# Fourteen value products for twenty, a turn moved from VectorE to TensorE in one batch, and splits on VectorE alone in another

## Chip, core and metric

The kernel runs on one core of a Trainium2 chip. The metric is the device time of one execution in microseconds (us); lower is better. TensorE is called PE, VectorE DVE, ScalarE ACT, GpSimd POOL, SyncE SP (its queue issues the DMAs).

## The reference

Three layers in a row, on 4 batches of 448 tokens. A causal attention with 12 heads of 64 columns; a mixing layer; and a second causal attention by 4 experts of which each token takes two.

```python
attn = softmax(causal(scale * q @ k.T)); x = attn @ v          # 12 heads, joined to 768 columns
theta = x @ w_theta
zr, zi = x * cos(theta), x * sin(theta)
u = x + w_tok_r @ zr + w_tok_i @ zi                            # over the 448 tokens
x = u + relu(u @ w_ch)
logits = x @ w_gate                                            # 4 experts, the best two are kept
for e in range(4):
    a = softmax(causal(scale * (x @ wq[e]) @ (x @ wk[e]).T))
    out += gate[e] * (a @ (x @ wv[e])) @ wo[e]
```

## The kernel before

Activations stand as features by tokens: six tiles `xt` of 128 x 448 per batch. Products that need accuracy are made of three: an operand is split into a rounded part and a rest, and hi x hi, hi x lo and lo x hi are added up in PSUM. So each of the big products of a batch (theta, channel, queries and keys) is 18 matrix instructions on 448 columns (`big`, line 877).

A batch runs through four stages: `attn1` (line 852, six pairs of heads), `mixing` (884), `project` (957: channel product, queries and keys, values with the gate's logits) and `attn2` (1052, two pairs of experts). `ORDER` (565) names the stages of all batches in the order in which they are recorded.

In `attn1` and `attn2` a pair of heads is a `Pair` (704). `scores` and `last` make the scores with queries on the partitions; DVE subtracts the mask and finds the row maximum, ACT takes the exponential, and ACT or POOL multiplies by the reciprocal sum. The result P lies in `pa` (2,048 columns: 16 blocks of 128 x 128, the causal part only). The values need P with keys on the partitions, so `turn` (772) turns it into `ph`: either PE transposes the 16 blocks into PSUM in four quarters of 512 columns and DVE or ACT copies each quarter out, or DVE transposes 32 x 32 blocks in place (two instructions of 1,024 columns) and 16 DMAs move the blocks. `BYDVE` (563) says for which pairs DVE does it. Then `two` (798, the loop at 828) multiplies by the values, query block by query block: 20 products a pair, 12 of 128 columns and 8 of 64. Each is two PE instructions, since these are plain 32-bit products.

Weights come as pairs of 32-bit halves of 64-bit numbers. In the first batch `widen` (641) makes them into a rounded part and a rest, by integer operations on DVE, a rounding copy on ACT, POOL or DVE, and a subtraction on POOL or DVE; the result is kept in DRAM (`scr`) and loaded as `unit` tiles by the later batches. There are six `unit` buffers and three `vt` buffers (values of the first attention). The seven tiles of token weights `wt` are widened in the first batch and stay. `split` (698) makes the two parts of an activation.

No engine's order is written by hand. Every operation is recorded with its due time, and `issue` (373) takes on each engine the recorded step that is due first and whose buffers are free. PE's own order comes from the table `RUNS` (568): so many steps of such a place of the program, then so many of another. `K` (566) holds the weights with which due times are worked out. A step recorded with a choice of engines (`copy`, `scale`, `combine`: letters s, v, g for ACT, DVE, POOL) goes to the one that would end it first. All are written out in `_emit` (537), so line 552 stands in nearly every row of the profile, and groups are told apart by tile names.

Of the kernel before, what the change touches and what calls it, by code (L numbers as in the profile page):

```python
# [17 lines left out]
OP = mybir.AluOpType  # L18
AX = mybir.AxisListType

B, H, S, D = 4, 12, 448, 64
DM = H * D
E = 4
P = 128
NK = DM // P
CW = [128, 128, 128, 64]
# [528 lines left out]
class Engine:  # L555
# [4 lines left out]
        return lambda *a, **kw: self._plan.add(self._name, method, *a, **kw)  # L560


BYDVE = {"a0": (), "a1": (3, 5, ), "a2": (0, 1, 2, 4, ), "a3": (0, 1, 2, 4, ), "c0": (0, 1, ), "c1": (0, ), "c2": (0, 1, ), "c3": ()}
ZBYDVE = [(), (), (), ()]
ORDER = ["a0", "m0", "a1", "p0", "c0", "m1", "a2", "p1", "c1", "m2", "a3", "p2", "c2", "m3", "p3", "c3"]
K = {"path": 1.7343403, "hop": 432.5379, "slack": -45.1941614, "war": 150.0, "ahold": 57315.6931, "free": -2869.0478,
    "warm": 16}
RUNS = [(1,2), (0,2), (2,1), (8,2), (3,4), (4,16), (14,1), (3,12), (5,1), (7,2), (9,1), (6,1), (14,1), (21,1),
# [23 lines left out]

# [3 lines left out]
def dense_sparse_attention_kernel(ctx: ExitStack, tc: tile.TileContext, qk, v, w64, w32, wo, wvg, wtok, out):  # L596
# [6 lines left out]
    plan = Plan(nc, tc)  # L603
    pe, act, dve, pool, sp = (Engine(plan, n) for n in ("tensor", "scalar", "vector", "gpsimd", "sync"))
# [14 lines left out]
    ident = const([P], F32, "ident")  # L619
# [21 lines left out]
    def widen(raw, n, hi, lo, by=1.0):  # L641


        e_, r_ = raw[:, :n, 1], raw[:, :n, 0].bitcast(U32)
        act.activation(e_.f32(), e_.f32(), AF.Copy, scale=REBIAS)
        e_ = e_.bitcast(U32)
        p_ = sbt([S], F32, "cmb")[:, :n]
        u_ = p_.bitcast(U32)
        dve.tensor_scalar(u_, e_, 3, 0x7FFFFFFF, op0=OP.logical_shift_left, op1=OP.bitwise_and)
        plan.claim(hi)  # L650
        dve.scalar_tensor_tensor(u_, r_, 29, u_, op0=OP.logical_shift_right, op1=OP.bitwise_or)
        dve.scalar_tensor_tensor(u_, e_, 0x80000000, u_, op0=OP.bitwise_and, op1=OP.bitwise_or)
        if by == 1.0:
            plan.copy(hi, p_, "sgv")
            plan.combine(lo, p_, hi.f32(), OP.subtract, "gv")
        else:
            plan.scale(hi, p_, by, "sgv")
            dve.scalar_tensor_tensor(lo, p_, by, hi.f32(), op0=OP.mult, op1=OP.subtract)
# [36 lines left out]
        parts = [t.rearrange("p h (k j) -> p h k j", j=width) for t in unit(u, DM // 2 if per == 2 else NVG, per, "unit")]  # L695
        return lambda a, k: parts[k // (NK // per)][:, a, k % (NK // per)]

    def split(dst_h, dst_l, src):
        plan.copy(dst_h, src, "svg")
        plan.combine(dst_l, src, dst_h.f32(), OP.subtract, "gv")  # L700

    UNIT = [14, 10, 0, 6]

    class Pair:

# [4 lines left out]
        def part(self, j, c):  # L710
            at = UNIT[c] + (c + 1) * j if c < 3 else UNIT[c]
            if self.by_dve:
                return self.by_key[:, at:at + c + 1]
            return self.p_[:, at * P:at * P + (128 * (c + 1) if c < 3 else S)]

        def softmax(self, sc_, p, n, m, col):
# [55 lines left out]
        def turn(self):  # L772
            plan.next()
            p_ = self.p_
            self.pt = pt = sbt([2048], F32, "ph")
            if self.by_dve:
                for at in (0, 1024):
                    dve.transpose(p_[:, at:at + 1024], p_[:, at:at + 1024])
                for a in range(4):
                    plan.group()  # L780
                    for b_ in range(4):
                        sp.dma_start(pt[32 * b_:32 * b_ + 32, 512 * a:512 * a + 512], p_[32 * a:32 * a + 32, 512 * b_:512 * b_ + 512])
                    plan.end_group()
            else:
                for i in range(4):
                    tp = pst("tp")
                    for n in range(4 * i, 4 * i + 4):
                        pe.transpose(tp[:, P * (n - 4 * i):P * (n - 4 * i + 1)], p_[:, P * n:P * n + P], ident)
                        if n == 4 * i:
                            plan.claim(pt)  # L790
                    plan.copy(pt[:, 512 * i:512 * i + 512], tp)

        def moving(self, at, q, n):
            if self.by_dve:
                return self.pt.rearrange("p (a u q) -> p a u q", a=4, u=16)[:, q // 32:(q + n) // 32, at]
            return self.pt[:, at * P + q:at * P + q + n]

    def two(pairs):

# [23 lines left out]
        for i, x in enumerate(pairs):  # L823
            plan.next()
            o_ = pst("tp")
            hl = [sbt([S], F32R, "hc") for _ in range(2)] if x.dest is None else []
            plan.group()
            for c in (2, 3, 1, 0):
                n = CW[c]
                for kc in range(c + 1):  # L830
                    for j in range(2):
                        if c == 3:
                            m = pairs[j].moving(UNIT[3] + kc, 64 * i, 64)
                        else:
                            m = x.moving(UNIT[c] + (c + 1) * j + kc, 0, P)
                        pe.matmul(o_[64 * j:64 * j + 64, c * P:c * P + n], x.vts[j][:, kc], m, start=(kc == 0), stop=(kc == c))
            plan.end_group()
            plan.completes(o_[:, :S])
            for tile_ in hl if x.dest is None else (x.dest,):
# [4 lines left out]
            h_, l_ = hl  # L844
# [39 lines left out]
    def mixing(b):  # L884
        hs = []
        xt = [x0[b, m] for m in range(NK)]
        for m in range(NK):
            t = sbt([2, S], F32R, "zt")
            h_, l_ = t[:, 0], t[:, 1]
            split(h_, l_, xt[m])  # L890
            hs.append((h_, l_))
        if b == 0:
            for k in range(7):
# [63 lines left out]
    def project(b):  # L957
        xt = [x0[b, m] for m in range(NK)]
        us = []
        for m in range(NK):  # L960
            t = sbt([2, S], F32R, "zt")
            split(t[:, 0], t[:, 1], xt[m])
            us.append((t[:, 0], t[:, 1]))
        for m in range(NK):
            o = big(6 + m, us)
# [3 lines left out]
        for m in range(NK):  # L969
            t = sbt([960], F32R, "zt")  # L970
            hi, lo = t[:, 0:S], t[:, 512:]
            split(hi, lo, xt[m])
            plan.combine(t[:, S:512], xt[m][:, 384:S], t[:, 384:S].f32(), OP.subtract, "gv")
            hs.append((hi, lo))
            both.append(t[:, 384:512])
        v2, qps = [], []
# [147 lines left out]
```

## Time and profile before

| | |
|---|---|
| three timed runs | 611.20, 611.82 (median), 612.81 us |
| the profiled execution's own time | 612.39 us |
| its span, first to last instruction | 610.6 us |
| busy: PE, DVE, ACT, POOL | 594.3, 419.9, 320.9, 126.8 us |
| mean granted clock of PE | 0.989 |
| instructions: PE, DVE, ACT, POOL | 4318, 1264, 862, 217 |

The time outside the span is 612.39 - 610.6 = 1.79 us. A granted clock of 1.00 is full speed. PE's instructions are pipelined, so the busy time of a stretch is the time in which any of them is under way.

### The profile page before, as it was taken

What the parts mean: (1) busy time and instruction counts of PE and PEld (TensorE: products, weight loads), DVE (VectorE), ACT (ScalarE), POOL (GpSimd) and SP (SyncE); (2) the same over time, 40 slices, a digit from 0 to 9 for tenths busy, and PEclk for the clock granted to TensorE, in tenths of its full rate; (3) what the DMA queues carried; (4) which work ended last, traced back from release to release, by engine and by line L of the source; (5) the groups of instructions that cost most, each with busy time, mean ns of one, the idle gap of its engine ahead of it and who ended that gap; (6) DMA issues with size and microseconds to landing.
All of it is one profiled execution on the core that took longest, in us unless ns stands there. A gap on an engine that the chain in (4) does not pass through costs nothing.

```text
span 610.6 us, 12498 instructions
## 1 busy us (share of the span) xinstructions
PE 594.3 (97%) x4318; PEld 515.8 (84%) x4318; DVE 419.9 (69%) x1264; ACT 320.9 (53%) x862; POOL 126.8 (21%) x217
## 2 busy tenths in 40 slices
PE   8999978999998999999999999999999999999987
PEld 6787866898897988988888887988898899999876
DVE  6999999999856876657454878648623976335360
ACT  6999887546554555145664676314634542200363
POOL 3554122521210324022020212302400201100020
PEclk9999996999998999999999999999999999999999
DMA  8457882379758756486586874456656756147442
GB/s 331 153 155 261 291 309 72 100 247 318 235 138 306 209 138 208 113 261 193 155 247 186 295 226 136 123 168 203 204 159 212 241 156 203 50 158 211 130 148 91
DMA packets 58622, 118.18 MB, mean 194 GB/s; under 512 B 8640, under 2 KB 22080, under 8 KB 58560
## 3 DMA queue, kind: packets, MB, share of 16 engines
q1 hardware_dynamic: 58560, 117.39, 61.0%
q8 instruction: 34, 0.56, 0.4%
q14 instruction: 28, 0.23, 0.1%
HBM read 80.37 MB, written 21.26 MB: 166 GB/s over the span
## 4 chain that ended last, share of the span: by engine, by line
PE 87%; ACT 6%; DVE 4%; issue 1%; DMA 1%; SPq 0%; POOL 0%; POOLq 0%; DVEq 0%; ACTq 0%
PE mm L552 61%; PE tp L552 27%; ACT pa L552 5%; DVE pa L552 2%; DVE cmb L552 1%; DMA unit<-scr 1%; DVE st L552 1%; ACT ph L552 0%; SPq L552 0%; DVE xt L552 0%; DVE zt L552 0%; ACT c L552 0%; DVE ph L552 0%; DVE tp L552 0%; ACT zt L552 0%
## 5 line engine op out<-in xcount | busy, mean ns | idle before, releaser
L552 PE MATMUL mm<-zt,unit 128*128 128x448 f32 x1152 | 244.2, 369 | 0.5 <-DVE zt L552 0.5
L552 PEld LDWEIGHTS mm<-zt,unit 128*128 128x128 f32 x1152 | 214.1, 188 | 25.4 <-issue 4.2
L552 ACT ACTIVATE pa<-pa,st 128x128 f32<-128x128 f32 (+4 forms) x229 | 110.1, 517 | 46.9 <-DVE st L552 45.5
L552 POOL TENSOR_SCALAR pa<-pa,st 128x128 f32<-128x128 f32 (+4 forms) x114 | 59.7, 540 | 220.1 <-DVE st L552 160.6
L552 PE MATMUL mm<-wt,zh 128*128 128x448 f32 x336 | 99.7, 376 | 4.9 <-DVE zt L552 3.5
L552 ACT ACTIVATE pa<-tp,st 128x128 f32<-128x128 f32 (+3 forms) x105 | 51.9, 505 | 42.5 <-DMA unit<-scr 17.9
L552 PEld LDWEIGHTS mm<-wt,zh 128*128 128x128 f32 x336 | 63.2, 192 | 11.6 <-issue 4.6
L552 PE MATMUL tp<-raw 64*128 64x256 f32 (+3 forms) x512 | 68.3, 438 | 0.2 <-DVE st L552 0.2
L552 PE MATMUL tp<-ph,vt 128*64 128x128 f32 (+1 forms) x1280 | 64.7, 258 | 2.1 <-DMA unit<-scr 2.1
L552 PEld LDWEIGHTS tp<-ph,vt 128*64 128x64 f32 x1280 | 57.7, 140 | 10.5 <-issue 3.7
L552 PE MATMUL mm<-wt,zl 128*128 128x448 f32 x168 | 62.4, 371 | 0.0
L552 PEld LDWEIGHTS tp<-raw 64*128 64x128 f32 (+1 forms) x512 | 38.3, 173 | 22.7 <-issue 8.7
L552 DVE CUSTOM_DVE_ANT_0 tp<-tp,mask 128x128 f32<-128x128 f32 (+3 forms) x105 | 45.6, 472 | 11.5 <-PE tp L552 10.4
L552 DVE CUSTOM_DVE_ANT_0 pa<-tp,mask 128x256 f32<-128x256 f32 (+3 forms) x119 | 47.2, 446 | 7.3 <-PE tp L552 6.9
L552 PE MATMUL tp<-ident,pa 128*128 128x128 f32 x272 | 36.2, 282 | 4.0 <-ACT pa L552 3.2
L552 DVE STREAM_TRANSPOSE pa<-pa 128x1024 f32<-128x1024 f32 x30 | 36.0, 1225 | 5.9 <-ACT pa L552 3.3
L552 PEld LDWEIGHTS tp<-ident,pa 128*128 128x128 f32 x272 | 31.1, 144 | 9.3 <-ACT pa L552 4.6
L552 POOL TENSOR_TENSOR zt<-xt,zt 128x448 fp32r<-128x448 f32 (+1 forms) x28 | 27.6, 999 | 53.5 <-DVE zt L552 48.4
L552 DVE SCALAR_TENSOR_TENSOR xt<-mm,xt 128x448 f32<-128x448 f32 x24 | 14.9, 623 | 34.3 <-PE mm L552 34.3
L552 DVE TENSOR_TENSOR zt<-xt,zt 128x448 fp32r<-128x448 f32 (+1 forms) x68 | 35.0, 553 | 0.5
L552 ACT ACTIVATE zh<-tp 128x512 fp32r<-128x512 f32 (+1 forms) x37 | 18.6, 545 | 30.4 <-PE tp L552 30.4
L552 PEld LDWEIGHTS mm<-wt,zl 128*128 128x128 f32 x168 | 32.0, 191 | 2.9 <-DVE zl L552 0.3
(104 smaller groups left out, 714.6 us busy)
## 6 DMA issues: line engine op xcount, KB each, us to landing
unit<-scr SPq DMA_DIRECT2D x96, 384.0 KB, 4.0
ph<-pa SPq DMA_DIRECT2D x240, 64.0 KB, 2.0
scr<-unit SPq DMA_DIRECT2D x32, 384.0 KB, 3.3
raw<-qk SPq DMA_DIRECT2D x24, 448.0 KB, 5.6
c<-w SPq DMA_DIRECT2D x24, 384.0 KB, 4.1
vt<-v SPq DMA_DIRECT2D x24, 256.0 KB, 4.2
unit<-scr SPq DMA_DIRECT2D x18, 260.0 KB, 3.5
out<-cmb SPq DMA_DIRECT2D x18, 224.0 KB, 2.6
```

Of the source, the lines that this page charges most:

```text
L552: getattr(getattr(self.nc, engine), name)(*args, **kw)
```

## The change

- `BYDVE`: pairs 3 and 5 of the second batch's first attention are turned by PE (before: DVE); of its second attention both pairs are turned by DVE (before: the first alone).
- The values: a pair's three full query blocks are taken together. For key block 0 one product covers 384 columns, for block 1 256, for block 2 128, and the last query block keeps its four of 64: 7 products for each of the two heads, 14 in all. For that the 16 blocks lie in another order in `pa` and `ph` (`LAND`, `TURNS`, `KEYED`).
- In the first batch the subtractions of `split` and of `widen` are DVE's alone.
- `RUNS` and `K` are new, so all engines' orders change.

```diff
-BYDVE = {"a0": (), "a1": (3, 5, ), "a2": (0, 1, 2, 4, ), "a3": (0, 1, 2, 4, ), "c0": (0, 1, ), "c1": (0, ), "c2": (0, 1, ), "c3": ()}
+BYDVE = {"a0": (), "a1": (), "a2": (0, 1, 2, 4, ), "a3": (0, 1, 2, 4, ), "c0": (0, 1, ), "c1": (0, 1), "c2": (0, 1, ), "c3": ()}
-K = {"path": 1.7343403, "hop": 432.5379, "slack": -45.1941614, "war": 150.0, "ahold": 57315.6931, "free": -2869.0478,
+K = {"path": 1.6514121, "hop": 476.4898, "slack": -38.9360047, "war": 176.7037, "ahold": 44547.6112,
...
-RUNS = [(1,2), (0,2), (2,1), (8,2), (3,4), (4,16), (14,1), (3,12), (5,1), (7,2), (9,1), (6,1), (14,1), (21,1),
+RUNS = [(0,2), (1,2), (2,1), (8,2), (3,16), (7,2), (4,16), (9,1), (6,1), (5,1), (11,16), (14,2), (10,1), (22,1),
...
-            plan.combine(lo, p_, hi.f32(), OP.subtract, "gv")
+            plan.combine(lo, p_, hi.f32(), OP.subtract, "v")
...
-    def split(dst_h, dst_l, src):
+    def split(dst_h, dst_l, src, by="gv"):
         plan.copy(dst_h, src, "svg")
-        plan.combine(dst_l, src, dst_h.f32(), OP.subtract, "gv")
+        plan.combine(dst_l, src, dst_h.f32(), OP.subtract, by)
...
+    TURNS = [((1, 4, 6, 9), (1, 11), 5, slice(0, 4, 3)), ((10, 11, 14, 15), (0, 16), 4, slice(2, 4)),
+             ((0, 2, 3, 5), (0, 6), 3, slice(0, 3, 2)), ((7, 8, 12, 13), (4, 14), 5, slice(3, 5))]
...
-                for i in range(4):
+                for ats, (lo, hi), width, pick in TURNS:
                     tp = pst("tp")
-                    for n in range(4 * i, 4 * i + 4):
+                    for n, at in enumerate(ats):
...
-                    plan.copy(pt[:, 512 * i:512 * i + 512], tp)
+                    plan.copy(to, tp.rearrange("p (x y q) -> p x y q", x=2, y=2))
...
-            for c in (2, 3, 1, 0):
-                n = CW[c]
-                for kc in range(c + 1):
-                    for j in range(2):
...
+            for kc in range(3):
+                for j in range(2):
+                    pe.matmul(o_[64 * j:64 * j + 64, kc * P:384], x.vts[j][:, kc], x.moving(kc, j, kc, 384 - kc * P), start=(kc == 0), stop=(kc == 2))
+            for kc in range(4):
+                for j in range(2):
+                    pe.matmul(o_[64 * j:64 * j + 64, 384:S], x.vts[j][:, kc], pairs[j].moving(3, j, kc, 64, 64 * i), start=(kc == 0), stop=(kc == 3))
...
-            split(h_, l_, xt[m])
+            split(h_, l_, xt[m], "gv" if b else "v")
```

What the order of instructions shows of it at three places (tile numbers are those of the program; a row with x2 is two products). First PE, the values of the first pair of heads; before:

```order
L552 MATMUL tp_304<-ph_212,vt_102 64x128 x6
L552 MATMUL tp_304<-ph_212,vt_102 64x64
L552 MATMUL tp_304<-ph_226,vt_102 64x64
...
L552 MATMUL tp_304<-ph_212,vt_102 64x64
L552 MATMUL tp_304<-ph_226,vt_102 64x64
L552 MATMUL tp_304<-ph_212,vt_102 64x128 x6
```

and now:

```order
L552 MATMUL tp_320<-ph_279,vt_102 64x384 x2
L552 MATMUL tp_320<-ph_279,vt_102 64x256 x2
L552 MATMUL tp_320<-ph_279,vt_102 64x128 x2
L552 MATMUL tp_320<-ph_211,vt_102 64x64
L552 MATMUL tp_320<-ph_279,vt_102 64x64
...
L552 MATMUL tp_320<-ph_211,vt_102 64x64
L552 MATMUL tp_320<-ph_279,vt_102 64x64
```

The first two products now read columns of all three full query blocks. Second PE, the first two products of the first batch's mixing (`mm` from `wt` and the turned `zh`, `zl`; three instructions for each of the seven token weights); before:

```order
L552 MATMUL mm_1376<-wt_1266,zh_1160 128x448 x2
L552 MATMUL mm_1376<-wt_1266,zl_1161 128x448
...
L552 MATMUL tp_1355<-ident_67,pa_1248 128x128 x3
L552 MATMUL tp_1426<-ident_67,pa_1248 128x128 x4
L552 MATMUL tp_1435<-ident_67,pa_1248 128x128 x4
L552 MATMUL mm_1445<-wt_1266,zh_1229 128x448 x2
L552 MATMUL mm_1376<-wt_1266,zh_1160 128x448 x2
L552 MATMUL mm_1376<-wt_1266,zl_1161 128x448
```

and now:

```order
L552 MATMUL mm_1367<-wt_1294,zh_1174 128x448 x2
L552 MATMUL mm_1367<-wt_1294,zl_1175 128x448
L552 MATMUL tp_1376<-ph_1311,vt_796 64x384 x2
...
L552 MATMUL tp_1404<-raw_725 128x256
...
L552 MATMUL tp_1412<-raw_969 128x384
...
L552 MATMUL mm_1367<-wt_1294,zh_1174 128x448
L552 MATMUL mm_1436<-wt_1294,zh_1189 128x448 x2
...
L552 MATMUL tp_1469<-ph_1275,vt_1134 64x384 x2
```

Scores (from `raw`) and values (from `ph`) of the second batch's first attention now stand after the first token weight's products, ahead of those of the seventh. Third SP's queue, at the end of the first batch's projection (`scr` from `unit` stores a widened tile, `unit` from `scr` loads one for the second batch); before:

```order
L552 DMA scr_5_463_2407<-unit_2323 256x1x260
L552 DMA c_464_2417<-wo 128x256
L552 DMA vt_2456<-v 128x512
L552 DMA unit_2462<-scr_0_185_919 128x768
L552 DMA unit_2469<-scr_1_189_944 128x768
```

and now:

```order
L552 DMA scr_5_474_2361<-unit_2352 256x1x260
L552 DMA unit_2423<-scr_0_104_494 128x768
L552 DMA unit_2434<-scr_1_172_807 128x768
L552 DMA unit_2455<-scr_0_210_998 128x768
```

The values `vt` of the last pairs are loaded earlier, and the second batch's first units follow the last store directly.

## Rows read from the trace of the kernel before

**Rows 1.** The page's head: span, busy share of each engine, DVE in 40 slices

```profile
span 610.6 us, 12498 instructions
...
PE 594.3 (97%) x4318; PEld 515.8 (84%) x4318; DVE 419.9 (69%) x1264; ACT 320.9 (53%) x862; POOL 126.8 (21%) x217
...
DVE  6999999999856876657454878648623976335360
```

**Rows 2.** Stretches: length, busy time (instructions) by engine, granted clock, DMA share, GB/s

```profile
0.00:40.00 40.00, 37.08 (x364) 27.64 (x365) 34.52 (x155) 34.51 (x112) 19.94 (x48) 1.00 0.67 231
...
87.30:100.00 12.70, 6.79 (x29) 4.51 (x26) 12.46 (x31) 9.43 (x24) 4.74 (x8) 0.73 0.45 159
...
187.10:195.48 8.38, 6.29 (x62) 4.45 (x61) 5.58 (x30) 3.73 (x13) 0.73 (x1) 0.80 0.97 326
195.48:586.75 391.27, 391.27 (x2734) 346.61 (x2738) 239.21 (x692) 170.76 (x458) 63.55 (x106) 1.00 0.60 182
586.75:591.87 5.12, 3.54 (x20) 2.29 (x20) 4.63 (x31) 3.02 (x9) 0.59 (x2) 1.00 0.81 265
```

**Rows 3.** Timeline of DVE, two stretches: start, us, instruction

```profile
58.60 0.55 DVE L552 SCALAR_TENSOR_TENSOR unit<-cmb,unit 128x384 fp32r<-128x384 f32 x1
59.07 0.55 DVE L552 SCALAR_TENSOR_TENSOR cmb<-c,cmb 128x384 uint32<-128x384 uint32 x1
...
104.59 0.62 DVE L552 TENSOR_TENSOR wt<-cmb,wt 128x448 fp32r<-128x448 f32 x1
105.13 0.55 DVE L552 SCALAR_TENSOR_TENSOR cmb<-c,cmb 128x384 uint32<-128x384 uint32 x1
```

**Rows 4.** Timeline of SP's queue and PE, 187.2 to 192.0 us

```profile
187.34 0.40 SPq L552 DMA_DIRECT2D vt<-v  x1
...
187.83 3.14 SPq L552 DMA_DIRECT2D unit<-scr  x6
...
191.90 0.38 PE L552 MATMUL tp<-ph,vt 128*64 128x128 f32 x2 [2.09 <-DMA unit<-scr]
```

**Rows 5.** The chain that ended last, in order of time: start, us, what

```profile
191.90 3.58 PE tp L552 x40
...
264.22 3.85 PE mm L552 x18
268.06 1.50 PE tp L552 x12
...
505.65 0.77 PE tp L552 x7
...
510.67 1.93 PE tp L552 x40
...
541.61 32.93 PE mm L552 x162
```

**Rows 6.** Groups of instructions by shape: count, busy us, mean ns of one, idle before

```profile
L552 PE MATMUL tp<-ident,pa 128*128 128x128 f32 x272 | 36.2, 282 | 4.0 <-ACT pa L552 3.2 <-POOL pa L552 0.8
...
L552 DVE STREAM_TRANSPOSE pa<-pa 128x1024 f32<-128x1024 f32 x30 | 36.0, 1225 | 5.9 <-ACT pa L552 3.3 <-DMA unit<-scr 2.2 <-POOL pa L552 0.4
...
L552 POOL TENSOR_TENSOR zt<-xt,zt 128x448 fp32r<-128x448 f32 x20 | 23.6, 1189 | 38.8 <-DVE zt L552 33.7 <-ACT zt L552 4.9
...
L552 DVE COPY ph<-tp 128x512 f32<-128x512 f32 x21 | 13.5, 679 | 0.5 <-PE tp L552 0.5
```

**Rows 7.** Timeline of POOL and DVE side by side, 109.0 to 114.3 us

```profile
109.14 1.17 POOL L552 TENSOR_TENSOR zt<-xt,zt 128x448 fp32r<-128x448 f32 x1
...
109.85 4.59 DVE L552 TENSOR_TENSOR zt<-zt,xt 128x448 f32<-128x448 f32 x6
...
110.62 1.19 POOL L552 TENSOR_TENSOR zt<-xt,zt 128x448 fp32r<-128x448 f32 x1 [0.32 <-ACT zt L552]
```

**Rows 8.** DMA issues: count, KB each, median us from issue to landing

```profile
unit<-scr SPq DMA_DIRECT2D x96, 384.0 KB, 4.0
...
vt<-v SPq DMA_DIRECT2D x24, 256.0 KB, 4.2
```

More of the change, by code (lines that the diff above doesn't have):

```diff
@@ L560, in __getattr__ @@
         return lambda *a, **kw: self._plan.add(self._name, method, *a, **kw)
-BYDVE = {"a0": (), "a1": (3, 5, ), "a2": (0, 1, 2, 4, ), "a3": (0, 1, 2, 4, ), "c0": (0, 1, ), "c1": (0, ), "c2": (0, 1, ), "c3": ()}
+BYDVE = {"a0": (), "a1": (), "a2": (0, 1, 2, 4, ), "a3": (0, 1, 2, 4, ), "c0": (0, 1, ), "c1": (0, 1), "c2": (0, 1, ), "c3": ()}
 ZBYDVE = [(), (), (), ()]
 ORDER = ["a0", "m0", "a1", "p0", "c0", "m1", "a2", "p1", "c1", "m2", "a3", "p2", "c2", "m3", "p3", "c3"]
-K = {"path": 1.7343403, "hop": 432.5379, "slack": -45.1941614, "war": 150.0, "ahold": 57315.6931, "free": -2869.0478,
-    "warm": 16}
-RUNS = [(1,2), (0,2), (2,1), (8,2), (3,4), (4,16), (14,1), (3,12), (5,1), (7,2), (9,1), (6,1), (14,1), (21,1),
[23 rows of a table removed]
+K = {"path": 1.6514121, "hop": 476.4898, "slack": -38.9360047, "war": 176.7037, "ahold": 44547.6112,
+    "free": -864.6802, "warm": 16}
+RUNS = [(0,2), (1,2), (2,1), (8,2), (3,16), (7,2), (4,16), (9,1), (6,1), (5,1), (11,16), (14,2), (10,1), (22,1),
[23 rows of a table added]
 @with_exitstack
@@ L696, in load_unit @@
         return lambda a, k: parts[k // (NK // per)][:, a, k % (NK // per)]
-    def split(dst_h, dst_l, src):
+    def split(dst_h, dst_l, src, by="gv"):
         plan.copy(dst_h, src, "svg")
-        plan.combine(dst_l, src, dst_h.f32(), OP.subtract, "gv")
+        plan.combine(dst_l, src, dst_h.f32(), OP.subtract, by)
     UNIT = [14, 10, 0, 6]
+    LAND = {(2, 0, 2): 1, (2, 0, 1): 4, (2, 1, 1): 6, (2, 0, 0): 9, (2, 1, 2): 10, (3, 0, 0): 11, (2, 1, 0): 14, (3, 0, 1): 15,
+            (3, 0, 2): 0, (3, 0, 3): 2, (1, 0, 1): 3, (1, 1, 1): 5, (0, 0, 0): 7, (1, 0, 0): 8, (0, 1, 0): 12, (1, 1, 0): 13}
+    TURNS = [((1, 4, 6, 9), (1, 11), 5, slice(0, 4, 3)), ((10, 11, 14, 15), (0, 16), 4, slice(2, 4)),
+             ((0, 2, 3, 5), (0, 6), 3, slice(0, 3, 2)), ((7, 8, 12, 13), (4, 14), 5, slice(3, 5))]
+    KEYED = {(0, 0): slice(0, 1), (1, 0): slice(1, 5, 3), (2, 0): slice(2, 9, 3),
+             (0, 1): slice(9, 10), (1, 1): slice(10, 5, -4), (2, 1): slice(11, 2, -4)}
     class Pair:
@@ L712, in part @@
             if self.by_dve:
-                return self.by_key[:, at:at + c + 1]
+                return self.by_key[:, KEYED[c, j] if c < 3 else slice(12, 16)]
             return self.p_[:, at * P:at * P + (128 * (c + 1) if c < 3 else S)]
@@ L784, in turn, with moving @@
             else:
-                for i in range(4):
+                units = pt.rearrange("p (u q) -> p u q", u=16)
+                rows = {at: UNIT[c] + ((c + 1) * j if c < 3 else 0) + kc for (c, j, kc), at in LAND.items()}
+                for ats, (lo, hi), width, pick in TURNS:
                     tp = pst("tp")
-                    for n in range(4 * i, 4 * i + 4):
-                        pe.transpose(tp[:, P * (n - 4 * i):P * (n - 4 * i + 1)], p_[:, P * n:P * n + P], ident)
-                        if n == 4 * i:
+                    for n, at in enumerate(ats):
+                        pe.transpose(tp[:, P * n:P * n + P], p_[:, P * rows[at]:P * rows[at] + P], ident)
+                        if n == 0:
                             plan.claim(pt)
-                    plan.copy(pt[:, 512 * i:512 * i + 512], tp)
-        def moving(self, at, q, n):
+                    to = units[:, lo:hi].rearrange("p (x y) q -> p x y q", y=width)
+                    to = to[:, (ats[0] - lo) // width:][:, :2, pick]
+                    plan.copy(to, tp.rearrange("p (x y q) -> p x y q", x=2, y=2))
+        def moving(self, c, j, kc, n, q=0):
             if self.by_dve:
-                return self.pt.rearrange("p (a u q) -> p a u q", a=4, u=16)[:, q // 32:(q + n) // 32, at]
-            return self.pt[:, at * P + q:at * P + q + n]
+                at = 12 + kc if c == 3 else [2 + 3 * kc, 11 - 4 * kc][j] - 2 + c
+                u = self.pt.rearrange("p (a u q) -> p a u q", a=4, u=16)
+                if c == 3:
+                    return u[:, q // 32:(q + n) // 32, at]
+                return u[:, :, at:at + n // P].rearrange("p a u q -> p u a q")
+            at = P * LAND[c, 0 if c == 3 else j, kc]
+            return self.pt[:, at + q:at + q + n]
     def two(pairs):
@@ L827, in two @@
             plan.group()
-            for c in (2, 3, 1, 0):
-                n = CW[c]
-                for kc in range(c + 1):
-                    for j in range(2):
[L832 to L836, printed above, removed]
+            for kc in range(3):
[4 more added lines that the diff above has]
+                    pe.matmul(o_[64 * j:64 * j + 64, 384:S], x.vts[j][:, kc], pairs[j].moving(3, j, kc, 64, 64 * i), start=(kc == 0), stop=(kc == 3))
             plan.end_group()
@@ L961, in project @@
             t = sbt([2, S], F32R, "zt")
-            split(t[:, 0], t[:, 1], xt[m])
+            split(t[:, 0], t[:, 1], xt[m], "gv" if b else "v")
             us.append((t[:, 0], t[:, 1]))
@@ L971, in project @@
             hi, lo = t[:, 0:S], t[:, 512:]
-            split(hi, lo, xt[m])
-            plan.combine(t[:, S:512], xt[m][:, 384:S], t[:, 384:S].f32(), OP.subtract, "gv")
+            split(hi, lo, xt[m], "gv" if b else "v")
+            plan.combine(t[:, S:512], xt[m][:, 384:S], t[:, 384:S].f32(), OP.subtract, "gv" if b else "v")
             hs.append((hi, lo))
```

46 rows, old and new, of the table RUNS are left out of this document.

## The prediction

> **What bounds the kernel now.** I read the page's head first: TensorE (PE) is busy 97% of the 610.6 us span, and VectorE (DVE) shows nines up to about a quarter of the span and sixes later [rows 1]. So the kernel has two parts: one in which DVE may hold PE up, and one in which PE is alone. The table by stretches says where PE loses time [rows 2]. From 195.48 to 586.75 us PE is busy in all 391.27 us: there only less PE work can help. Three places lose. From 0 to 40 us 2.9 us are idle. From 87.3 to 100 us PE is busy in 6.79 of 12.70 us, at a granted clock of 0.73, while DVE is busy in 12.46. From 187.1 to 195.48 us it is busy in 6.29 of 8.38 us at a clock of 0.80. At 586.75 a last gap has 3.54 of 5.12 us busy.
>
> What the second place waits for stands in DVE's timeline [rows 3]: it widens the seven tiles of token weights, and the last subtraction into `wt` starts at 104.59 and ends at 105.21 us. It does nothing else meanwhile that could be dropped: its rows follow each other without a gap, an operation on 448 columns every 0.54 us, on 384 every 0.47. The third place is a DMA [rows 4]: the values product at 191.90 waited 2.09 us. It reads a `vt` whose load was issued only at 187.34, behind other transfers on SP, and six unit loads follow it from 187.83. Then its 40 instructions take 3.58 us, where another pair's forty take 1.93 at full clock [rows 5]. Together that place loses 2.09 + 1.65 = 3.7 us.
>
> **The prices.** In steady stretches of the chain [rows 5] 18 products of 448 columns take 3.85 us with the switch in front, 162 in a row 32.93 (203 ns each), a pair's twelve score instructions 1.50, its forty value instructions 1.93, seven transposes 0.77 (110 ns each). With these I count PE's queue, and with the spacings of rows 3 and the means of [rows 6] less their overlap DVE's queue, ahead of a given row of the order. The difference, DVE's work ahead less PE's work ahead, is the least by which PE must lag there.
>
> **The change part by part, against the profiled execution** (610.6 us span, 612.39 in all, so 1.79 outside the span; it stands 0.57 above the median of 611.82).
>
> *The order in the first batch.* Before, PE first needs the seventh token weight with 83.5 us of its own work done, and DVE has 102.6 us queued up to that weight: a lag of 19.1. That is right: the trace has this weight at 105.2, 2.6 later than DVE's count, since DVE starts late and idles a little. In the changed order two value groups and one and a half score groups of the second batch's attention stand between the first mixing products, so 90.8 us of PE work lie ahead of the first use of the seventh weight. DVE's queue up to it counts 103.3: more subtractions for splits, but fewer casts of turned z and of x, which went to ScalarE and GpSimd. The lag is 12.5, which is 6.6 less. The next place that can bind is the last split of the mixed x before the channel product: 117.1 us of PE work against 130.6 of DVE's, a lag of 13.5. So 19.1 - 13.5 = 5.6 us are gained, if DVE never waits for PE. I take **-5.6**; the ends are -6.6 (first place alone) and 0 (the new order only shifts the wait).
>
> *VectorE alone splits.* Over the kernel DVE gets 20 more two-input operations, 13 of 448 and 7 of 384 columns: 10.3 us by rows 3. Those that fall before the two places are in the counts above. GpSimd loses them, 1.19 us each where they have 448 columns [rows 6]. What the two engines cost each other is bounded by [rows 7]: beside two GpSimd subtractions six DVE products take 4.59 us where six spacings of 0.54 make 3.24, so 0.7 us for each GpSimd operation at most. Eight such operations stand ahead of the seventh weight before and none after: 0 to 5.4 us. I take 0, because the count of DVE without any such cost already comes out only 2.6 us early, and DVE's start explains that.
>
> *The values.* A pair's 20 products become 14, so 40 instructions become 28, with the same 4,096 columns (before: 24 of 128 and 16 of 64). If an instruction costs a fixed time f and c per column, 40f + 4096c = 1.93 us and f + 448c = 203 ns give f = 2.3 ns: 12 x 2.3 = 28 ns a pair, 0.9 us over 32 pairs. If the columns run at one per cycle of 2.4 GHz, the level that the granted clock of 1.00 stands for, they take 1.71 us and f is 5.6 ns: 2.1 us. I take **-1.5**.
>
> *The turns.* Batch two's two pairs go from DVE to PE, and one pair of its second attention the other way: 16 more transposes at 110 ns, **+1.8** on PE, which is the bound there. DVE loses two transposes of 1.2 us [rows 6], off the path. The row says 110 ns each. The Trainium skill ("TensorE: Matmul & The Clock Gate", Part 4: PE-mode transpose) tells of about 275 ns for a transpose in one kernel's context; by that the turns would be an estimated 4.4 us and the sum 2.6 higher. The trace speaks against it: 272 of them are busy for 36.2 us [rows 6], 133 ns each with their waits.
>
> *The hand-over from the first projection to the second batch.* The place of 3.7 us goes: the first attention is over earlier, and no value group stands there. In its place the first unit of the next batch takes the buffer of the first of the six value-weight tiles. Between the last read of that buffer and the first use of the unit PE has 4.2 us of work. Its load needs about 0.5 us to issue (six in 3.14) and 4.0 to land [rows 4, 8]: a wait of 0.3. Two later `vt` loads have 4.9 and 4.3 us, and need 0.4 + 4.2: 0 and 0.3. Such waits run from 0 to the 3.7 of before, each; I take **1.5** for the three. So -3.7 + 1.5 = **-2.2**.
>
> *The end.* The eight last score instructions now stand ahead of the final value products, so PE has less to do in the gap at 586.75 (about 2.4 us), but the gate's chain on DVE is shorter by two subtractions of 448 columns, 1.1 us. 5.12 - 1.1 - 2.4 leaves 1.6 idle, as now: 0.
>
> Sum: -5.6 - 1.5 + 1.8 - 2.2 = -7.5, which makes 604.9 for the profiled execution and 604.3 by the median.
>
> **The rivals.**
> *DVE pays in full (slower).* The second batch's attention that was moved ahead needs DVE too, for its masked subtractions and copies. If PE therefore finds none of it ready, and the 10.3 us of extra subtractions all delay the seventh weight, the first batch costs 10.3 more in place of 5.6 less: 604.3 + 15.9 = 620.2. For it: DVE's nines [rows 1]. Against it: DVE's queue up to that weight is only 0.7 us longer. It decides if the weight comes later than 105.2 + 7.3 = 112.5 us. 7%.
> *The hand-over stays.* A late load costs 3.7 again, where I have 0.3: 607.7. For it: 4.2 us of cover against 4.5 of need, and DMA engines at 0.97 there [rows 2]. Against it: nothing is queued ahead of the load. 15%.
> *Values wait for the whole turn.* Before, a pair's first twelve value instructions need the first quarters of its turned P alone. Now the first product takes columns from all four, so PE waits for one more copy, 0.68 us on DVE [rows 6]. Where the values follow the turn closely, in the six pairs of the first batch and the two at the end, this is 8 x 0.68 = 5.4: 609.7. Against it: another pair's turn or scores mostly stand between. 13%.
> *The engines free each other.* If the 0.7 us of rows 7 hold for all eight operations, DVE reaches the seventh weight 5.4 us sooner, and PE gains as much: 598.9. Against it: the count above needs no such cost. 10%. The Trainium skill ("SBUF — State Buffer", Two separate sides) states that GpSimd and a two-input DVE operation lock each other out for a whole instruction; by GpSimd's own time that would be an estimated 9 us for the eight, and a time near 595. Rows 7 show about half.
>
> **How the numbers follow.** The forecast holds 55%. About 0.3% (1.8 us) is what a measurement of this kernel can tell from no change. Forecast, hand-over, freed engines and part of the copies' case are faster: 85%. The rest of the copies' case, with a smaller gain at the start, is no change: 8%. Slower 7%. The range 598.5 to 610.5 leaves out the slow rival and the outer ends of two others.
>
> **What would show it.** Right: DVE still full up to about 130 us; the last write of `wt` near 106 us; PE idle less between 87 and 110 us and its clock there nearer 1; no low clock near 190 us; 28 value instructions in about 1.88 us. Wrong: the last `wt` after 112 us, a wait of more than 1.5 us for a `unit` or `vt` load, or a new idle stretch of PE after 200 us.

## The result and the profile after

Four timed runs of the changed kernel give a median of 605.08 us (604.36 to 605.74), beside 612.24 us of the kernel before (611.20 to 612.81): a ratio of 0.9884, 95% interval 0.9860 to 0.9908. The profiled execution took 605.35 us, with a span of 603.6. The forecast of 604.3 us was right in sign and within 0.8 us, inside its range. Two of its gains were taken too small, one too large, and a loss was not foreseen; they cancelled.

The page's head of the changed kernel answers to [rows 1]:

```profile
span 603.6 us, 11721 instructions
...
PE 590.8 (98%) x3950; PEld 499.1 (83%) x3950; DVE 414.0 (69%) x1268; ACT 323.0 (54%) x874; POOL 107.2 (18%) x201
...
DVE  6899999999847889355638878537735866324261
...
PEclk9999999999999999999999999999999999999999
```

VectorE is as full in the first quarter as before. GpSimd lost 20 us of work, PE 368 instructions. The granted clock is nine tenths of full speed or more in every slice, and 1.000 in the mean. The stretches of the changed kernel, cut where [rows 2] cut those of before as far as the stages still lie there (length, busy us by engine, granted clock, DMA share, GB/s):

```profile
0.00:40.00 40.00, 36.40 (x315) 26.11 (x316) 31.89 (x147) 33.62 (x109) 18.01 (x45) 1.00 0.63 224
87.30:100.00 12.70, 11.60 (x92) 8.00 (x92) 12.67 (x40) 12.60 (x34) 2.45 (x5) 1.00 0.54 207
...
187.10:195.48 8.38, 8.38 (x42) 7.63 (x42) 6.51 (x39) 6.01 (x20) 3.04 (x6) 1.00 0.96 342
195.48:575.00 379.52, 377.72 (x2421) 323.69 (x2421) 232.02 (x656) 162.47 (x436) 64.23 (x105) 1.00 0.61 186
```

From 87.3 to 100 us PE is busy for 11.60 us where it was for 6.79, at 1.00 instead of 0.73. At the hand-over it is busy throughout. From 195.48 to 575 us 1.8 us are idle, where none were. DVE's timeline shows the two places that the prediction's lag came from:

```profile
104.97 0.61 DVE L552 TENSOR_TENSOR wt<-cmb,wt 128x448 fp32r<-128x448 f32 x1
...
132.45 1.15 DVE L552 TENSOR_TENSOR zt<-xt,zt 128x448 fp32r<-128x448 f32 x2
```

The seventh token weight is written at 105.58, nearly the 105.21 of before [rows 3], and the last split of the mixed x at 133.60. VectorE did not get faster. PE has more to do meanwhile. Before, the longest row of waiting in PE's timeline was this, followed by three more of 0.5 to 1.1 us at a low clock:

```profile
91.97 0.64 PE L552 MATMUL mm<-wt,zh 128*128 128x448 f32 x2 [3.50 <-DVE zt L552]
```

Now PE's timeline has four short ones for token weights, with another pair's values (28 instructions) between:

```profile
97.38 0.47 PE L552 MATMUL mm<-wt,zh 128*128 128x448 f32 x1 [0.60 <-DVE wt L552]
...
98.53 0.47 PE L552 MATMUL mm<-wt,zh 128*128 128x448 f32 x1 [0.47 <-ACT wt L552]
98.98 1.98 PE L552 MATMUL tp<-ph,vt 128*64 128x384 f32 x28
...
104.76 0.47 PE L552 MATMUL mm<-wt,zh 128*128 128x448 f32 x1 [0.60 <-DVE wt L552]
```

To find where the 7.0 us of span come from, I subtract from each stretch the PE instructions in it at their steady prices (those of the prediction). What is left is **PE's loss**: waiting, slow clock, and pipeline starts. It is 21.7 us before and 14.9 after from 0 to 150 us (-6.8); 0.3 and -0.1 from there to 180 (-0.4); 3.8 and 0.2 from 180 to 200 (-3.6); 1.6 and 4.7 from 200 to 560 (+3.1); 5.3 and 5.8 behind that (+0.5). This makes -7.2 for the 7.0 of the spans. The prediction's prices put 0.3 us more work into the changed kernel (1.8 for 16 more transposes, less 1.5 for the values), and roundings are the rest; no matmul record is missing, since 3950 is 4318 less 12 for each of 32 pairs, plus 16. But the values turn out to save 0.6 and not 1.5 (e12 below), so the work is 1.2 us more and the losses must fall by more. With 1.91 us for a pair's 28 instructions and each instruction counted in one stretch alone, the five differences are -7.6, -0.3, -3.5, +3.0 and +0.3, together -8.1. The losses given below are good to about 1 us.

### The profile page after: what moved, and what is told of

Its sections match the earlier page's. It is cut to its first block, busy times and chain, and to the rows that moved or that the text cites. A ratio compares the mean times of both kernels' runs of the same rounds, so it can differ in the third digit from the quotient of the medians.

```text
span 603.6 us, 11721 instructions
## 1 busy us (share of the span) xinstructions
PE 590.8 (98%) x3950; PEld 499.1 (83%) x3950; DVE 414.0 (69%) x1268; ACT 323.0 (54%) x874; POOL 107.2 (18%) x201
## 4 chain that ended last, share of the span: by engine, by line
PE 82%; DVE 8%; ACT 7%; DMA 1%; issue 1%; POOL 0%; SPq 0%; POOLq 0%; DVEq 0%; ACTq 0%
PE mm L552 56%; PE tp L552 26%; ACT pa L552 4%; DVE pa L552 2%; DVE zt L552 2%; ACT ph L552 1%; DMA unit<-scr 1%; ACT zt L552 1%; DVE cmb L552 1%; DVE st L552 1%; DVE tp L552 1%; ACT L552 0%; DVE ph L552 0%; DVE sm L552 0%; DMA ph<-pa 0%
## 5 line engine op out<-in xcount | busy, mean ns | idle before, releaser
L552 ACT ACTIVATE pa<-pa,st 128x256 f32<-128x256 f32 (+4 forms) x238 | 115.2, 526 | 17.2 <-DVE st L552 16.1
L552 POOL TENSOR_SCALAR pa<-pa,st 128x384 f32<-128x384 f32 (+4 forms) x112 | 60.4, 556 | 213.8 <-DVE st L552 147.6
L552 PE MATMUL tp<-raw 64*128 64x384 f32 (+3 forms) x512 | 67.6, 439 | 0.5 <-DVE st L552 0.5
L552 ACT ACTIVATE pa<-tp,st 128x256 f32<-128x256 f32 (+3 forms) x98 | 48.4, 506 | 28.0 <-DVE st L552 19.4
L552 PEld LDWEIGHTS tp<-ph,vt 128*64 128x64 f32 x896 | 41.9, 137 | 23.4 <-issue 13.2
L552 PE MATMUL tp<-ph,vt 128*64 128x64 f32 (+3 forms) x896 | 60.7, 291 | 0.0
L552 DVE CUSTOM_DVE_ANT_0 tp<-tp,mask 128x256 f32<-128x256 f32 (+3 forms) x98 | 42.2, 474 | 11.3 <-PE tp L552 7.4
L552 ACT ACTIVATE zh<-tp 128x384 fp32r<-128x384 f32 (+1 forms) x42 | 20.5, 537 | 35.6 <-PE tp L552 35.5
L552 ACT ACTIVATE cmb<-tp 128x448 f32<-128x448 f32 x15 | 8.1, 542 | 57.6 <-PE tp L552 57.6
L552 DVE TENSOR_TENSOR xt<-xt,mm 128x448 f32<-128x448 f32 x24 | 14.8, 616 | 29.7 <-PE mm L552 29.7
```

The source lines that it names most:

```text
L552: getattr(getattr(self.nc, engine), name)(*args, **kw)
```

## The experiments

There are two kinds. In the first eight the edit is made in the program and the planner orders all engines anew. In the last four every engine's order is kept, and only the named instructions change. The kernel before was run with each set, with medians from 611.06 to 613.27, so kernels are compared by their ratio to it; the changed kernel's is 0.9884.

**e1_splits_shared**: the changed kernel, with GpSimd allowed to take subtractions of the first batch again. The edit also lets it take that batch's products with the cosine, which neither of the two kernels does.

```diff
-            plan.combine(lo, p_, hi.f32(), OP.subtract, "v")
+            plan.combine(lo, p_, hi.f32(), OP.subtract, "gv")
...
-            split(h_, l_, xt[m], "gv" if b else "v")
+            split(h_, l_, xt[m], "gv")
...
-                    plan.combine(z[:, 0], z[:, 0], xt[j], OP.mult, "gv" if b else "v")
+                    plan.combine(z[:, 0], z[:, 0], xt[j], OP.mult, "gv")
```

> The changed kernel, but GpSimd may again take split subtractions in the first batch. Theory (the lag of PE behind DVE in the first batch sets the gain; counted from the order of instructions as DVE work less PE work ahead of the worst place): the seventh token weight stays at a lag of 12.8 (12.5 in the change), but the worst place, a turned z, comes to 18.7 in place of 13.6, so up to 5.1 us more: 605 to 610. Rival 1 (who subtracts does not matter): 605 within 1. Rival 2 (GpSimd's subtractions hold DVE up by 0.7 us each as well): over 610.

616.54 us (615.10 to 618.65), ratio 1.0068 (1.0043 to 1.0094): 11 us more than the changed kernel. That looks like the engines holding each other up, but it is only part of it. PE's loss from 0 to 150 us is 26.4, 11.5 more. Three VectorE operations are stretched beside GpSimd's work, two beside subtractions and one beside such a product, by 0.97, 1.14 and 0.97 us: 3.1. VectorE's queue in the new plan has 5.1 us more ahead of a product (the table at the end of this section). And PE's timeline has one long wait, for ACT:

```profile
110.13 3.68 PE L552 MATMUL tp<-ph,vt 128*64 128x384 f32 x28 [6.32 <-ACT pa L552]
```

The exponential that it waits for has its input from VectorE at 104.93, but in ACT's timeline sine operations, between two loads of a function table, come first:

```profile
103.83 1.28 ACT L552 ACT_TABLE_LOAD   x1
105.12 0.58 ACT L552 ACTIVATE zt<-zt 128x448 f32<-128x448 f32 x1
...
108.33 1.28 ACT L552 ACT_TABLE_LOAD   x1
109.62 0.37 ACT L552 ACTIVATE pa<-tp,st 128x128 f32<-128x128 f32 x1
```

The two engines can also hold each other up the other way round. Here GpSimd takes two products, the first of them 4.37 us long, beside VectorE operations from SBUF to SBUF that are as short as ever:

```profile
107.83 5.46 POOL L552 TENSOR_TENSOR zt<-zt,xt 128x448 f32<-128x448 f32 x2 [9.58 <-ACT zt L552]
109.51 1.16 DVE L552 TENSOR_TENSOR wt<-cmb,wt 128x448 fp32r<-128x448 f32 x2
```

So the freedom given to GpSimd also changed what the other engines do first, and e1 can't say what sharing costs. That is why e10 to e13 keep the order.

**e4_parts_old_order**: the changed kernel's 14 products and VectorE's splits, with `RUNS`, `K` and `BYDVE` of before.

```diff
-RUNS = [(0,2), (1,2), (2,1), (8,2), (3,16), (7,2), (4,16), (9,1),
+RUNS = [(1,2), (0,2), (2,1), (8,2), (3,4), (4,16), (14,1), (3,12),
```

> The changed kernel with the turns, the table of PE's order and the weights of before: 14 products and the first batch's splits on DVE alone. Theory: the lag at the worst place is 26.2 by the count where before had 20.0, so the first batch is 6 us longer than before's: 616 to 619. Rival (the parts bring the gain, the order is a detail): 605 to 609.

614.06 us, ratio 1.0025 (1.0011 to 1.0040), between the two. PE's loss from 0 to 150 us is 25.6, but the planner's reshuffle took the hand-over's loss from 3.8 to 1.0.

**e5_order_turns_only**: the reverse, the kernel before with `RUNS`, `K` and `BYDVE` of the changed one.

> The kernel before with the new table of PE's order, the new weights and the new turns, but 20 products and shared splits. Theory: the lag is 16.0 (before 20.0, the change 13.6), the hand-over's 3.7 us are gone but for 1, the turns cost 1.8: 612.2 - 4.0 - 2.7 + 1.8 = 607 to 608. Rival (the parts bring the gain): 611 to 614.

612.49 us, ratio 1.0001 (0.9987 to 1.0015), a miss, and inside the rival's range. With e4 it says that neither the parts nor the order with the turns gain anything alone, when the planner works out the rest anew. The hand-over loses only 0.1 us, yet the first 150 us lose 21.5, 5.5 more than the count (the table below). The longest wait in PE's timeline there is for GpSimd:

```profile
111.94 1.40 PE L552 MATMUL mm<-wt,zh 128*128 128x448 f32 x2 [2.43 <-POOL wt L552]
```

But the GpSimd rounding that it waits for had itself waited for VectorE, so this doesn't explain the excess:

```profile
111.31 0.57 POOL L552 TENSOR_SCALAR wt<-cmb 128x448 fp32r<-128x448 f32 x1 [4.68 <-DVE cmb L552]
```

**e2_turns_back**: the changed kernel, with the second batch's pairs 3 and 5 turned by VectorE again.

```diff
-BYDVE = {"a0": (), "a1": (), "a2"
+BYDVE = {"a0": (), "a1": (3, 5), "a2"
```

> The changed kernel, but the second batch's pairs 3 and 5 are turned by DVE again (32 transposes less on PE, both pairs of the second attention stay on DVE). Theory: by the count DVE's work ahead of the first batch's worst place grows to a lag of 28.2 from 13.6, while PE has 3.5 us less to do: 605.1 + 14.6 - 3.5 = about 616, at least 611. Rival (PE is the bound, so less work on PE is a gain): 601.6.

624.09 us, ratio 1.0216 (1.0201 to 1.0231): 20 us more, the dearest of all edits. PE's timeline has one wait for a token weight:

```profile
114.78 0.74 PE L552 MATMUL mm<-wt,zh 128*128 128x448 f32 x1 [10.88 <-ACT wt L552]
```

VectorE's own time is not all of it. A turn by VectorE sends 16 block moves through SP's queue, and here the loads of the last four token weights (`zt` from `wtok`) stand behind them. This is SP's queue in e2, then in the changed kernel:

```profile
87.58 11.73 SPq L552 DMA_DIRECT2D ph<-pa  x16
99.41 1.97 SPq L552 DMA_DIRECT2D zt<-wtok  x4
```

```profile
82.18 6.24 SPq L552 DMA_DIRECT2D zt<-wtok  x6
```

The last of these loads are issued from 99.41 us on, where the changed kernel has issued them all by 88.42, and e2's chain that ended last runs through SP's queue and such a load up to 104.92 us. How many of the 20 us that makes is not shown.

**e8_first_batch_new** and **e9_first_batch_old**: the changed kernel with a table put together from both. e8 has the new order up to the second batch's mixing and the old one behind it (and one pair of the second batch's second attention on PE, as before); e9 has the old order first (with pairs 3 and 5 on VectorE) and the new one behind.

> The changed kernel with the new table up to the hand-over to the second batch and the table of before from there on; the second attention of batch two as before (one pair turned by PE). Theory (first batch and hand-over are the whole gain): 605 to 607, with 1.8 us for 16 transposes. Rival (the new order of later batches brings some of it): 608 to 611.

> The changed kernel with the table of before up to the hand-over and the new one from there on; the second batch's pairs 3 and 5 turned by DVE as before. Theory: the lag is 24.5 by the count (before 20.0), and the hand-over's 3.7 us are back, while PE has 3.5 us less transposes than the change: 612 to 617. Rival (the new order of later batches brings the gain): 605 to 608.

Both missed: 614.50 us, ratio 1.0062 (1.0049 to 1.0074), and 610.62 us, ratio 0.9986 (0.9975 to 0.9997). Up to 150 us e8 loses 13.7 us, like the changed kernel, and at the hand-over 0.2; what spoils it is a wait behind the seam, in the second batch:

```profile
321.46 2.60 PE L552 MATMUL tp<-hc,c 128*128 128x448 f32 x6 [6.68 <-DVE c L552]
```

e9 loses 25.4 us up to 150 us, as the old order should, but has 3.5 us less to do on PE, and its hand-over loses 1.0. The times of such tables don't measure a part; their stretches do.

**e6_one_group_earlier**: the kernel before, with the values group of the hand-over three entries earlier in the table.

```diff
-(75,2), (72,18), (74,12), (58,1), (73,18)
+(58,1), (75,2), (72,18), (74,12), (73,18)
```

> The kernel before with one entry of PE's table moved: the values of the second batch's pair 4 stand three entries earlier, ahead of the first score group of the second attention, so that the buffer of the values for pair 5 is free sooner and its load stands ahead of the output weights' on SP. Theory (a late load of values causes the 3.7 us at 187 to 195): the load is issued about 1.1 us sooner, which is held up by the three stores ahead of it; PE waits 1.1 us less and may keep its clock: 609.5 to 611. Rival (the unit loads behind it are what PE waits for): 612.2 within 0.5.

613.14 us, ratio 1.0038 (1.0025 to 1.0051), a miss for both. There is no usable trace of it, so where its time went stays open.

**e3_twenty_products**: the changed kernel with the 20 products and their old order.

> The changed kernel, but with 20 value products a pair in the old order of query blocks (new layout kept). Theory: a group of 40 instructions takes 1.93 us and one of 28 takes 1.91, so 32 groups cost 0.6 us more, and the count of the lag gives 14.7 in place of 13.6: 1.1 more; together 606 to 607. Rival (values now wait for all four quarters of a turn, and 20 products would not): 603 or less. Rival of the prediction (1.5 us from the products alone): 606.6 with no change of the lag.

607.77 us, ratio 0.9929 (0.9908 to 0.9950): 2.7 us more, of which 1.7 are a greater loss up to 150 us (16.6). Is that the products or the planner? The next one tells.

**e12_twenty_same_order**: the same, with every other instruction of all engines at its place.

```diff
+            step = plan.steps[-1]
+            step.calls = []
+            for c in (2, 3, 1, 0):
...
+                        step.calls.append(("tensor", "matmul", (o_[64 * j:64 * j + 64, c * P:c * P + CW[c]], x.vts[j][:, kc], m),
```

> The changed kernel with the order of every engine as it is, but each pair's 14 value products again written as the 20 of the kernel before (same columns, same place in PE's queue, same 32 pairs). The prediction's price of the products is 1.5 us (0.9 to 2.1): 606.6 (606 to 607.2). By the rows of the changed kernel, where a pair takes 1.91 us for 1.93, it is 32 x 0.02 = 0.6: about 605.7, which the runs can hardly tell from 605.1. If the twenty, whose first products need one quarter of the turned P alone, spare PE waits for the rest of the turn, it comes out at or below 605.

606.23 us, ratio 0.9893 (0.9870 to 0.9915), the changed kernel's within the interval, which is too wide to tell 0.6 us from 1.5; the profiled span is 603.0 us, not longer than 603.6. So most of e3's excess was the planner's. The groups by shape are these, first of e12, then of the changed kernel:

```profile
L552 PE MATMUL tp<-ph,vt 128*64 128x128 f32 x768 | 51.9, 275 | 0.0
L552 PE MATMUL tp<-ph,vt 128*64 128x64 f32 x512 | 20.3, 222 | 0.0
```

```profile
L552 PE MATMUL tp<-ph,vt 128*64 128x384 f32 x128 | 27.1, 502 | 0.0
L552 PE MATMUL tp<-ph,vt 128*64 128x64 f32 x512 | 20.3, 222 | 0.0
L552 PE MATMUL tp<-ph,vt 128*64 128x256 f32 x128 | 19.2, 379 | 0.0
L552 PE MATMUL tp<-ph,vt 128*64 128x128 f32 x128 | 12.4, 273 | 0.0
```

Busy time counts overlaps, so sums of groups of different length aren't compared; the chain is plainer, first of e12, then of the changed kernel at the same places:

```profile
458.83 1.93 PE tp L552 x40
...
502.04 1.93 PE tp L552 x40
```

```profile
459.47 1.91 PE tp L552 x28
...
502.45 1.91 PE tp L552 x28
```

Forty take 1.93, as they did before [rows 5], and 28 take 1.91.

**e11_eight_to_vector**: the kernel before, order kept; the eight subtractions ahead of the seventh token weight that GpSimd does are emitted on VectorE.

```diff
+            if step.order in self.marked:
+                self.nth += 1
+                if self.nth in (1, 2, 3, 4, 5, 7, 8, 9):
+                    engine = "vector"
```

> The kernel before with every engine's order as it is, except that the eight subtractions ahead of the seventh token weight that GpSimd does go to VectorE, at the same places. Theory A, VectorE's queue sets the lag: 4.3 us more ahead of the seventh weight, a lag of 23.4 for 19.1, about 616 (615 to 617.5). Theory B, each of them had held VectorE up by 0.7 us or more: 0.16 to 0.61 less each, 607 to 611. No difference (611 to 613): what they cost each other is about the 0.54 us that the operation takes on VectorE, and then the splits alone are worth nothing in either order.

616.57 us (615.69 to 616.89), ratio 1.0078 (1.0055 to 1.0101): 5.2 more, theory A. DVE's timeline has the last token weight 3.8 us later than before [rows 3] (this kernel's own line for emission is 559):

```profile
108.42 0.61 DVE L559 TENSOR_TENSOR wt<-cmb,wt 128x448 fp32r<-128x448 f32 x1
```

**e10_eight_to_gpsimd**: the mirror image, the changed kernel with the same eight on GpSimd (`engine = "gpsimd"`).

> The changed kernel with every engine's order as it is, except that eight of the thirteen subtractions of 448 columns that stand ahead of the seventh token weight on VectorE go to GpSimd, at the same places (the same eight, by their number, that GpSimd does in the kernel before: five of x, three of the token weights). GpSimd has nothing else to do there. Theory A, VectorE's queue sets the lag and sharing costs it nothing: 8 x 0.54 = 4.3 us less on VectorE ahead of the binding places, so about 601 (600 to 602.5). Theory B, a GpSimd subtraction holds VectorE up for longer than the 0.54 us that it takes off it (0.7 us by the rows of the kernel before, at most its own 1.15): 8 x 0.16 = 1.3 to 8 x 0.61 = 4.9 us more, 606 to 610. Between the two, 603 to 605.5, only part of them stands on the path.

606.71 us, ratio 0.9925 (0.9899 to 0.9951): not 4 us faster but 1.6 slower by the medians, 2.5 by the ratios (the intervals just overlap), theory B. VectorE and GpSimd side by side show why:

```profile
41.13 1.58 DVE L559 SCALAR_TENSOR_TENSOR cmb<-c,cmb 128x384 uint32<-128x384 uint32 x1
41.16 2.56 POOL L559 TENSOR_TENSOR zt<-xt,zt 128x448 fp32r<-128x448 f32 x2
42.63 1.49 DVE L559 SCALAR_TENSOR_TENSOR unit<-cmb,unit 128x384 fp32r<-128x384 f32 x1
...
43.85 1.27 POOL L559 TENSOR_TENSOR zt<-xt,zt 128x448 fp32r<-128x448 f32 x1
44.05 1.28 DVE L559 TENSOR_SCALAR unit<-cmb 128x384 fp32r<-128x384 f32 x1
45.26 0.54 DVE L559 CUSTOM_DVE_ANT_0 pa<-tp,mask 128x384 f32<-128x384 f32 x1
```

Operations that take 0.55 and 0.35 us alone take 1.58, 1.49 and 1.28 beside GpSimd's subtractions. Seven of the eight hold VectorE up so, by 0.74, 1.04, 0.95, 0.94, 0.76, 0.98 and 0.95 us: 6.4 us, against 8 x 0.54 = 4.3 saved. In the kernel before only one of the same eight did, by 0.95. There they stand beside masked subtractions, copies out of PSUM and VectorE's transposes, which they don't hold up:

```profile
93.71 2.36 DVE L552 STREAM_TRANSPOSE pa<-pa 128x1024 f32<-128x1024 f32 x2
...
94.52 1.14 POOL L552 TENSOR_TENSOR wt<-cmb,wt 128x448 fp32r<-128x448 f32 x1
```

The Trainium skill ("SBUF — State Buffer", SBUF: two separate sides) states an exclusive lock between a GpSimd operation and a VectorE operation that has two SBUF inputs or runs in a two-port mode. The trace of e10 agrees for the rows with two inputs in SBUF, which are held (0.74 to 1.04 us), and for the rows that read PSUM, which are not. Whether the one-input row at 44.05 was in such a mode no trace here shows.

**e13_casts_to_gpsimd**: the changed kernel, order kept; nine one-input roundings ahead of the seventh token weight go from VectorE to GpSimd.

```diff
+        if step.order in self.casts and step.engine == "vector" and self.nth < 13:
+            step.calls = [c for o in step.options if o[0] == "gpsimd" for c in o[2]]
```

> The changed kernel with the order of every engine as it is, but the nine roundings (five of 384 and four of 448 columns) that VectorE does ahead of the seventh token weight go to GpSimd, at the same places. They have one input each. Theory A, a GpSimd instruction with one large input does not hold VectorE up: 5 x 0.27 + 4 x 0.30 = 2.6 us less on VectorE ahead of the binding places, 602.5 to 604, less where PE or a subtraction waits for the longer way round by GpSimd. Theory B, any GpSimd instruction holds VectorE's work on the same memory up, by its own 0.5 us: 9 x 0.5 - 2.6 = 1.9 more, 605.5 to 607.5. No difference (604.5 to 605.5): the lag of the changed kernel is not VectorE's queue any more.

605.30 us, ratio 0.9876 (0.9854 to 0.9899): no difference. The last token weight stands even later:

```profile
105.89 0.61 DVE L563 TENSOR_TENSOR wt<-cmb,wt 128x448 fp32r<-128x448 f32 x1
```

Of the 2.6 us taken off VectorE 2.0 came back as stretched operations beside six of the nine (by 0.25 to 0.43 us); that the rest goes to waits for the rounded part on its longer way is likely, not shown. No run beats the changed kernel by more than the measurement can tell.

**The count against the runs.** For each kernel the prediction's count (VectorE's work ahead less PE's, the largest up to 130 us), and PE's loss from 0 to 150 us:

| kernel | count, us | loss, us |
|---|---|---|
| before | 20.0 | 21.7 |
| changed | 13.6 | 14.9 |
| e8, new first batch | 13.6 | 13.7 |
| e3, twenty products | 14.7 | 16.6 |
| e10, eight on GpSimd | 9.3; with 6.4 of holds 15.7 | 15.6 |
| e11, eight on VectorE | 24.3 | 24.7 |
| e9, old first batch | 24.5 | 25.4 |
| e4, parts in old order | 26.2 | 25.6 |
| e2, turns back | 28.2 | 32.5 |
| e5, order and turns | 16.0 | 21.5 |
| e1, splits shared | 18.7; with 3.1 of holds 21.8 | 26.4 |

In eight of the eleven the loss is the count within 2 us, in e10 only with the holds, which come from the same trace. The three others have more: e1 a wait for ACT, e2 the late loads behind SP's block moves, and e5's excess of 5.5 stays open.

## Why the prediction was right, and where it was not

- **The order in the first batch, -5.6: right, a little more (-6.8, or -7.6 with the measured price of the values).** The mechanism is the one given: VectorE's queue ends no earlier (105.58 for a predicted 106), and PE's queue ahead of the seventh weight is longer. Two steps on the way were not right. The prediction set 19.1, the lag at the seventh weight, against 13.5; the largest lag of before is 20.0, and its own rule gives 6.5. And VectorE's queue did not stay as long because of fewer casts. In the traces it has eight subtractions (4.3 us) and four roundings more ahead of the seventh weight, but five copies of turned quarters (0.6 us each) and both block transposes (2.4) less. e8 shows that the new order up to the second batch's mixing brings all of it, e9 and e11 that the old order with VectorE's splits loses 24 to 25 us. From e11 (1.0078) to the changed kernel (0.9884) lie 1.9%, about 12 us, with the eight subtractions on VectorE in both; order, turns, products and hand-over share them.
- **VectorE alone splits, 0 for the sharing.** In the sum this was right, since the count of before held: only one of its eight GpSimd subtractions held VectorE up. But the reason was incomplete. What a shared operation costs depends on its neighbour: about 0 beside work that reads PSUM, near 1 us beside a two-input operation. So moving the eight to VectorE costs 5.2 us in the old order (e11) and gains about 2 in the new one (e10). The rival of the freed engines fell for the same reason: ahead of the seventh weight there were 0.95 us to free, not 5.4.
- **The values, -1.5: mis-sized.** Measured is 0.02 us a pair, 0.6 in all, in e12 at the same places too. The step that failed is the fixed time f for each instruction: in a steady queue these products cost little but their columns, and f is about 0.02 us / 12 = 1.7 ns where the prediction took 2.3 to 5.6. The rival that values wait for the whole turn had no price either, since e12, whose first products need one quarter, is not faster.
- **The turns, +1.8, "off the path" for VectorE: the second half was wrong.** The price on PE held (32 transposes in 3.79 us, 118 ns each). But two of VectorE's transposes stood right ahead of the token weights, 2.36 us at 93.71, so they were on the path, and the prediction's reading that VectorE does nothing there that could be dropped failed on the same row. They were in the count, which is why the sum didn't suffer. Of the 6.6 us by which the prediction's lag at the seventh weight shrank, 4.2 came with the turns: 2.4 less for VectorE, and 16 transposes (1.8) more of PE's work ahead of it. e2 puts the turns back and loses 20 us, far more than the transposes themselves: by the count VectorE's queue there grows by 14.6, with a new plan, and loads come late behind SP's block moves. Up to 150 us it loses more (32.5) than the old order with the same turns (e9, 25.4), so the order is not shown to gain without the turns.
- **The hand-over, -2.2: too small (-3.6).** The place went as argued, but the 1.5 us of new waits for loads did not come. PE is busy for all 8.38 us at 1.00. From 180 to 200 us the runs with the new order up to there lose at most 0.3 us, e4 and e9 (old table, planned anew) 1.0, e11 (old order kept) 3.9. e2's 4.8 in that stretch is another thing: its first batch ends later, and PE still waits there for widened weights (1.60 us at 194.20, 0.97 at 196.02). At its own hand-over, from 202.28 us, PE waits for no load, although VectorE turns the pairs. That moving one group cures the place is not shown (e6).
- **Not foreseen: +3.1 us of small waits between 200 and 560 us.** I had said that a new idle stretch there would speak against me. There are four of 0.3 to 0.7 us, 1.8 in all; where the rest of the 3.1 went was not traced. One of them in PE's timeline:

```profile
332.66 12.58 PE L552 MATMUL mm<-zt,unit 128*128 128x448 f32 x60 [0.47 <-DVE zt L552]
```

- **The end, 0: nearly right.** A wait of 1.73 us at 584.81 stands for the 1.58 of before.

In the sum, the order and the hand-over brought 2.6 us more than forecast (3.3 with the measured price of the values), the products 0.9 less, and the small waits took 3.1. That these cancel to 0.8 us is luck.

## What to carry to other kernels

Where two engines run side by side from the same start, count the work queued ahead of a product on both: the difference is the least the faster one must wait, and it can be cut by putting other work ahead of that product as well as by making the slower engine faster. Before sharing an operation with GpSimd, look at what VectorE does beside it: in these traces a 32-bit subtraction was free beside reads of PSUM and block transposes, and dearer than it saved beside other operations from SBUF to SBUF. Where a planner orders the engines, measure a part with the order kept; an edit that lets it plan anew measures its luck too (much of e1's 11 us and of e3's 2.7 was that).

## What the runs showed of the hardware that I had not expected

- In e10 a GpSimd subtraction of 448 columns held a VectorE operation with two SBUF inputs, or a one-input operation from SBUF to SBUF, up by 0.74 to 1.04 us, and masked subtractions from PSUM (0.55 us beside it, 0.54 without) and, in the kernel before, block transposes (2.36 us for two, beside it) not at all.
- GpSimd's one-input roundings (0.5 to 0.6 us alone) stretched VectorE's operations too, six of nine by 0.25 to 0.43 us, about the 0.27 to 0.30 that each took off it.
- It also went the other way: in e1 a GpSimd product of 448 columns took 4.37 us, where a GpSimd operation of this size takes 1.14 alone, beside VectorE operations from SBUF to SBUF that were not stretched.
- Joining products of 128 columns to products of up to 384 saved about 1.7 ns for each instruction that went.
